# Attention with a soft mixture of experts on one core: the order of two key transfers in the last batch, and the tile at which one weight unit is sent for

## The chip, the cores and the metric

The kernel runs on one core of one Trainium2 chip. The metric is the device time of one execution in microseconds (us), lower is better. The time before is the median of three runs, 250.34 us (247.84 to 250.55). The profile comes from a further, profiled execution that has a time of its own, 251.09 us.

## The reference

Windowed causal attention (window 128, linear bias by head) over 8 batches, 8 heads, 576 positions and head size 64; its output, seen as 4608 tokens of 512 features, goes through a soft mixture of 8 experts with 4 slots each.

```python
scores = scale * np.matmul(q, k.transpose(0, 1, 3, 2))
mask = (rel >= 0) & (rel < window)
scores = np.where(mask, scores + bias[None], -1000000000.0)
attn = np.exp(scores - max); attn = attn / (sum + 1e-09)
x = (attn @ v) as [tokens, heads * head_dim]
logits = x @ phi                       # 4608 x 32
d = softmax of logits over the tokens; slot_input = d.T @ x
slot_out[e] = relu(slot_input[e] @ w1[e]) @ w2[e]     # 8 experts, F = 1024
out = (softmax of logits over the slots) @ slot_out
```

## The kernel before

The work is cut into 36 tiles of 128 tokens. A batch of 576 positions has four tiles `t` = 0 to 3 of 128 queries, and the 64 queries left over of two neighbouring batches make a fifth, `t` = 4. So even batches have four tiles and odd ones five. Tiles are counted here from 0 in the order in which they run: tile 10 is the eleventh and belongs to batch 2, tiles 31 to 35 are those of the last batch (batch 7), which runs in the order `t` = 1, 4, 2, 3, 0. Batch 0 starts at tile 0, batch 1 at 4, batch 2 at 9, batch 3 at 13, batch 6 at 27.

One pass of the main loop, "period k", works on several tiles at once. TensorE (PE) transposes the probabilities of tile k-1 (L319) and the finished tokens of tile k-3 (L387), multiplies tile k-2 by its values (L355, L367), and ends with the scores of tile k+1 (L263). The scores come in two halves `g` = 0 and 1, each with 16 matmuls and a PSUM buffer of its own. VectorE (DVE) merges the window (L277), finds the row maxima into `nb` (L286), and divides by the row sums (L378, L381). ScalarE (ACT) does the exponentials (L301) and copies out of PSUM (L322, L390). GpSimd (POOL) cuts the window's corners (L339, L342). Every fourth tile the logits and the running slot sums are added (L400, L438, L450).

All loads of the main loop are issued by SyncE (SP) in one hand-written order. An issue waits for the buffer it writes to be free and for the transfer eight places ahead of it to have landed, and what stands behind a waiting issue waits too. In period k SP gets, in this order:

- `weights(k)`: units of expert weights, 512 KB each, 64 in all, from tile 3 on. Ahead of each unit `hold` issues a 4-byte transfer into `beat` that reads the row maxima `nb` of one half of tile k, so the unit can't leave before DVE has them. Tiles in `BOTH` send for two units, one behind each half; the others for one, behind the first half, or the second if they are in `LATE`.
- `after_values(k-2)`: loads of values (`va`) into slots that PE has just freed.
- `loads(k+1)`, behind the scores of tile k+1: the queries (`q_t`) of tile k+3, and part of the keys (`k_t`). Keys come in blocks of 64 positions, 128 KB each; `k_part(b, i, e)` loads blocks i to e-1 of batch b, and there are `NB` = 9 in a batch.

In the last batch the second half of tile 32 (`t` = 4) reads blocks 6, 7 and 8, and tile 33 (`t` = 2) reads blocks 2 to 5. The kernel before sends for blocks 4 and 5 in `loads(30)` and for blocks 6 to 8 in `loads(31)`.

Behind the main loop the slots' inputs go through the experts: `hidden` (L774) with the first 32 units, `experts` (L810) with the other 32, and `combine` (L831, L837) writes the output. Of the 64 units 38 go behind holds; the other 26 are sent for at the end of the loop and in the tail.

Of the kernel before, what the change touches and what calls it, by code (L numbers as in the profile page):

```python
# [37 lines left out]
NB = S // KB  # L38
# [7 lines left out]
GAPS = (1, 3)  # L46
WFIRST = 3
LATE = (4, 5, 21, 25, 29, 30)
BOTH = (31, 32, 33, 34, 35)
CUTS = (0, 128, 256, 384, 512)  # L50
NM = len(CUTS) - 1
MW = [CUTS[m + 1] - CUTS[m] for m in range(NM)]
# [15 lines left out]
def tile_attn_softmoe(  # L68
# [74 lines left out]
    def hold(ap):  # L143
        i = len(held)
        held.append(ap)
        nc.sync.dma_start(beat[0:1, i:i + 1], ap[0:1, 0:1])

    def load_weight():
        n = loaded[0]
        loaded[0] += 1  # L150
        m, e, k = units[n]
        if NW <= n < NW + len(place):
            wt[units[n]] = place[n - NW]
        else:
            wt[units[n]] = wpool.tile([P, UW], F32, tag="w", name=f"w{n}")
        nc.sync.dma_start(wt[units[n]], (w1d, w2d)[m][e, :, UW * k:UW * (k + 1)])

    st = {}
    last = B - 1
# [403 lines left out]
    def k_part(b, i, e):  # L563
        return (load_k, (b, i, e))

    def loads(k):
        b, t = tiles[k]
        now = []
        if k + 2 < n:
            now.append((load_q, (k + 2,)))  # L570
        if k < 4:
            now.append((load_v, ()))
        if t == 0 and 0 < b < last:
            now.append(k_part(b, 4, 6))
        if t == 1:
            now.append(k_part(b, 6, NB))
        if b % 2 == 0 and t == 2:
            now.append(k_part(b + 1, 0, 2))
        if b % 2 == 0 and (t == 3 if b + 1 < last else t == 2):
            now.append(k_part(b + 1, 2, 4))  # L580
        if b + 1 == last and t == 3:
            now.append(k_part(last, 4, 6))
        if b % 2 and b < last and t >= 3:
            now.append(k_part(b + 1, 2 * t - 6, 2 * t - 4))
        issue(now)
# [11 lines left out]
    def issue(items):  # L597
        for fn, a in items:
            fn(*a)

    def weights(k):
        gates = (0, 1) if k in BOTH else (k in LATE,)
        for g in gates if k >= WFIRST else ():
            hold(st[k, g]["nb"])
            load_weight()

    for q in range(NQ - 1):
        k = 4 * q + 6
# [13 lines left out]
    with tc.manual_schedule(engines=ORDERED):  # L622
        scores(0, 0)
        idle_work(GAPS[0])
        scores(0, 1)
        loads(0)
        for k in range(n):
            if k:
                chain(k, 0)
            else:  # L630
                for us in (LO, HI):
                    merge(k, 0, us)
                    rowmax(k, 0, us)
                    expo(k, 0, us)
            chain(k, 1)
            weights(k)
            for _ in range(2):
                filler()
# [32 lines left out]
            if k + 1 < n:  # L671
                scores(k + 1, 0)
                scores(k + 1, 1)
                loads(k + 1)
# [312 lines left out]
```

## Time and profile before

| | us |
|---|---|
| median of three runs | 250.34 |
| lowest and highest | 247.84, 250.55 |
| the profiled execution, its own time | 251.09 |
| span of its instructions | 249.4 |
| PE busy in the span | 234.5 |
| DVE, ACT, POOL busy | 176.8, 165.6, 94.5 |

The 1.7 us between own time and span lie around the program. In the profile an instruction's row has its start, how long it took, engine, line, tiles, and in brackets how long its engine sat idle before it and what ended that by the profile. "SPq" rows are issues of transfers. A share of the DMA is the mean busy share of 16 DMA engines in a stage.

### The profile page before, as it was taken

How to read it: one execution, taken by the hardware profiler on the slowest of the kernel's cores; microseconds unless marked ns; L12 is line 12 of the kernel's file. 1: busy time of each engine (PE TensorE's matmuls, PEld its weight loads, DVE VectorE, ACT ScalarE, POOL GpSimd, SP SyncE). 2: the span in 40 equal slices, each digit the busy share in tenths (PEclk: the TensorE clock that was granted, in tenths of full speed). 3: DMA queues.
4: the chain of work that ended last, by engine and by line, in shares of the span. 5: the costliest groups of instructions: out<-in, count | busy, mean ns of one | idle time of the engine just before them, and what ended most of it. 6: DMA issues, size and time to landing. Idle time of an engine off the chain costs nothing. (4 is left out here: it accounts for less than half of the span.)

```text
span 249.4 us, 12344 instructions
## 1 busy us (share of the span) xinstructions
PE 234.5 (94%) x4867; PEld 175.6 (70%) x4868; DVE 176.8 (71%) x971; ACT 165.6 (66%) x473; POOL 94.5 (38%) x235
## 2 busy tenths in 40 slices
PE   6989999998999999999999999979997999999982
PEld 2668887886788778787788788768876423766640
DVE  0787888986998898798798899778886412244451
ACT  2698987987888888797797979849762310033441
POOL 2038455723651765086077608537550010000000
PEclk9999999999999999999999999999999999999985
DMA  6798887796897588888876989988899999977997
GB/s 175 250 289 273 264 315 216 257 335 216 273 297 255 167 292 262 292 287 252 298 230 212 288 239 330 303 314 293 257 329 369 409 408 410 407 277 307 354 387 277
DMA packets 28505, 72.72 MB, mean 292 GB/s; under 512 B 3358, under 2 KB 3872, under 8 KB 28448
## 3 DMA queue, kind: packets, MB, share of 16 engines
q1 hardware_dynamic: 27728, 71.11, 83.1%
q10 hardware_dynamic: 720, 0.84, 1.2%
q8 instruction: 38, 0.62, 1.0%
q14 instruction: 19, 0.16, 0.2%
HBM read 62.49 MB, written 9.44 MB: 288 GB/s over the span
## 5 line engine op out<-in xcount | busy, mean ns | idle before, releaser
L301 ACT ACTIVATE area<-sq,nb 128x128 f32<-128x128 f32 x288 | 89.4, 400 | 4.0 <-DVE nb L286 2.9
L342 POOL TENSOR_SCALAR_AFFINE_SELECT area<-area 64x256 f32<-64x256 f32 x112 | 46.3, 413 | 85.3 <-ACT area L322 76.9
L286 DVE CUSTOM_DVE_ANT_0 sq<-s,cst 128x128 f32<-128x128 f32 x224 | 51.8, 287 | 7.7
L322 ACT COPY area<-pt 128x512 f32<-128x512 f32 x71 | 41.9, 593 | 20.6 <-PE pt L319 17.6
L263 PE MATMUL s<-kq 64*64 64x192 f32 (+2 forms) x1152 | 51.6, 310 | 3.6 <-DVE nb L286 2.1
L339 POOL TENSOR_SCALAR_AFFINE_SELECT area<-area 64x256 f32<-64x256 f32 x112 | 45.5, 416 | 5.8
L263 PEld LDWEIGHTS s<-kq 64*64 64x64 f32 x1152 | 39.6, 135 | 9.4 <-DVE nb L286 3.8
L319 PE MATMUL pt<-unit_r,area 128*128 128x128 f32 x288 | 44.3, 278 | 0.0
L355 PE MATMUL xp<-va,area 128*64 128x65 f32 x1120 | 41.1, 224 | 1.3 <-issue 1.3
L355 PEld LDWEIGHTS xp<-va,area 128*64 128x64 f32 x1120 | 35.9, 137 | 7.5 <-issue 5.8
L319 PEld LDWEIGHTS pt<-unit_r,area 128*128 128x128 f32 x288 | 32.2, 140 | 7.1 <-ACT area L301 4.6
L277 DVE COPY_PREDICATED s<-cst,s 128x256 f32<-128x256 int32 (+1 forms) x73 | 30.6, 419 | 6.7 <-PE s L263 6.6
L381 DVE TENSOR_TENSOR xs<-xp,rs 128x256 f32<-128x256 f32 x70 | 26.6, 420 | 1.2
L390 ACT COPY xs<-xq 128x512 f32<-128x512 f32 (+1 forms) x36 | 20.9, 585 | 6.0 <-PE xq L387 5.8
L286 DVE DVE_READ_ACCUMULATOR2_ANT nb<- 128x1 f32 x288 | 23.8, 83 | 0.0
L387 PE MATMUL xq<-unit_r,xs 128*128 128x128 f32 x142 | 21.9, 278 | 1.2 <-DVE xs L381 0.9
L837 DVE COPY ob<-po 128x384 f32<-128x384 f32 x24 | 12.5, 554 | 13.7 <-PE po L831 12.9
L367 PEld LDWEIGHTS xp<-va,area 64*64 64x64 f32 x864 | 15.2, 133 | 7.4 <-issue 6.4
L837 ACT COPY ob<-po 128x384 f32<-128x384 f32 x24 | 10.5, 481 | 14.0 <-PE po L831 13.9
L367 PE MATMUL xp<-va,area 64*64 64x65 f32 x864 | 19.0, 224 | 0.0
L387 PEld LDWEIGHTS xq<-unit_r,xs 128*128 128x128 f32 x142 | 15.9, 141 | 3.3 <-PE pt L319 2.4
L286 DVE CUSTOM_DVE_ANT_0 sq<-s,fine 128x128 f32<-128x128 f32 x64 | 14.9, 287 | 1.9
(109 smaller groups left out, 232.8 us busy)
## 6 DMA issues: line engine op xcount, KB each, us to landing
w<-w SPq DMA_DIRECT2D x48, 512.0 KB
out<-ob SPq DMA_DIRECT2D x24, 384.0 KB
kq<-q_t SPq DMA_DIRECT2D x34, 256.0 KB
va<-v_n SPq DMA_DIRECT2D x32, 260.0 KB
kq<-k_t SPq DMA_DIRECT2D x24, 256.0 KB
kq<-k_t SPq DMA_DIRECT2D x8, 384.0 KB
kq<-w SPq DMA_DIRECT2D x4, 512.0 KB
area<-w SPq DMA_DIRECT2D x4, 512.0 KB
```

Of the source, the lines that this page charges most:

```text
L263: nc.tensor.matmul(parts[par][half[c], jh, KB * o:WIN], lhsT=qt[rows, j], rhs=keys[rows, i:i + 3 - o, j], start=(t > 0 and jh == 0), stop= ...
L277: nc.vector.copy_predicated(window(k, g, us, 0, KB), bc(mask_le, 1, len(range(4)[us])), window(k, g, us, P, KB))
L286: nc.vector.tensor_tensor_reduce(out=s["sq"][:, u], in0=window(k, g, u, 0, P), in1=bias[:, u] if tiles[k][1] else zero.to_broadcast([P, P] ...
L301: nc.scalar.activation(dst, s["sq"][:, u].rearrange("p (a w) -> p a w", a=2), AF.Exp, bias=s["nb"][:, u:u + 1], scale=-1.0)
L319: nc.tensor.transpose(s["pt"][:, u], s["p4"][:, u], ident)
L322: copy(pas[k % 2][:, g].rearrange("p a j m -> p (a j m)"), st[k, g]["pt"].rearrange("p u w -> p (u w)"))
L339: nc.gpsimd.affine_select(dst, pa, [[0, NPAIR], [-1, KB]], ALU.is_gt, 0.0, base=0, channel_multiplier=1)
L342: nc.gpsimd.affine_select(dst, pa, [[0, NPAIR], [1, KB]], ALU.is_ge, 0.0, base=0, channel_multiplier=-1)
L355: nc.tensor.matmul(x[par][half[g], j], lhsT=pas[k % 2][:, g, par, j], rhs=v[:, par, j], start=(j == 0), stop=(t == 0 and j == NPAIR - 1))
L367: nc.tensor.matmul(x[par][half[g], j], lhsT=pps[k % 2][rows, g, j], rhs=v, start=False, stop=(j == NPAIR - 1))
L381: nc.vector.tensor_tensor(x[:, par], xp[par][:, :, 0:D], bc(rs[:, par], 2, D), op=ALU.mult)
L387: nc.tensor.transpose(st["xq", k][:, P * j:P * j + P], xns[k % NXN][:, P * j:P * j + P], ident)
```

## The change

Two things are edited, each in a rule that sets SP's order. Nothing else changes: the instructions of PE, DVE, ACT and POOL stand in the same order as before, and the 64 weight units come in the same order.

```diff
 LATE = (4, 5, 21, 25, 29, 30)
-BOTH = (31, 32, 33, 34, 35)
+NONE = (10,)
+BOTH = (12, 31, 32, 33, 34, 35)
...
         if t == 1:
-            now.append(k_part(b, 6, NB))
+            now.append(k_part(b, 6, NB) if b < last else k_part(b, 4, 6))
...
         if b + 1 == last and t == 3:
-            now.append(k_part(last, 4, 6))
+            now.append(k_part(last, 6, NB))
...
     def weights(k):
         gates = (0, 1) if k in BOTH else (k in LATE,)
-        for g in gates if k >= WFIRST else ():
+        for g in gates if k >= WFIRST and k not in NONE else ():
             hold(st[k, g]["nb"])
             load_weight()
```

Since a line is added at the top, lines of the changed kernel behind it have numbers that are one higher.

**First place, SP from period 10 to period 12.** `beat` and `w_` are a hold and its unit, `va` values, `q_t` queries, `k_t` keys (128x512 is two blocks, 128x768 three). Before:

```order
L146 DMA beat<-nb 1x1
L156 DMA w_1128<-w 128x1024
L197 DMA va<-v_n 128x520 x2
L180 DMA kq<-q_t 128x512
L187 DMA kq<-k_t 128x512
L146 DMA beat<-nb 1x1
L156 DMA w_1252<-w 128x1024
L204 DMA va<-v_t 128x520
L180 DMA kq<-q_t 128x512
L187 DMA kq<-k_t 128x512
L146 DMA beat<-nb 1x1
L156 DMA w_1357<-w 128x1024
```

Now:

```order
L198 DMA va<-v_n 128x520 x2
L181 DMA kq<-q_t 128x512
L188 DMA kq<-k_t 128x512
L147 DMA beat<-nb 1x1
L157 DMA w_1249<-w 128x1024
L205 DMA va<-v_t 128x520
L181 DMA kq<-q_t 128x512
L188 DMA kq<-k_t 128x512
L147 DMA beat<-nb 1x1
L157 DMA w_1354<-w 128x1024
L147 DMA beat<-nb 1x1
L157 DMA w_1357<-w 128x1024
```

The first hold and unit (period 10) are gone from the top; period 12 ends with two holds and two units in place of one. From there on SP is level with the kernel before.

**Second place, SP from `loads(30)` to the weights of period 31**, with the semaphores that each issue waits for. Before:

```order
L180 DMA kq<-q_t 128x512 [waits DMAHW3_49,PE_49]
L187 DMA kq<-k_t 128x512 [waits DMAHW4_49]
L146 DMA beat<-nb 1x1 [waits DMAHW5_49,DVE_49]
L156 DMA w_3415<-w 128x1024 [waits DMAHW6_49]
L197 DMA va<-v_n 128x520 [waits DMAHW7_49,PE_49]
L180 DMA kq<-q_t 128x512 [waits DMAHW0_49,PE_49]
L187 DMA kq<-k_t 128x768 [waits DMAHW1_49]
```

Now:

```order
L181 DMA kq<-q_t 128x512 [waits DMAHW3_49,PE_49]
L188 DMA kq<-k_t 128x768 [waits DMAHW4_49]
L147 DMA beat<-nb 1x1 [waits DMAHW5_49,DVE_49]
L157 DMA w_3415<-w 128x1024 [waits DMAHW6_49]
L198 DMA va<-v_n 128x520 [waits DMAHW7_49,PE_49]
L181 DMA kq<-q_t 128x512 [waits DMAHW0_49,PE_49]
L188 DMA kq<-k_t 128x512 [waits DMAHW1_49]
```

The three blocks and the two blocks have changed places. A transfer signals on the semaphore of the one whose place it takes, so the three blocks signal on DMAHW1 before and on DMAHW4 now.

**Third place, PE at the scores of tiles 32 and 33** (`s_0` and `s_1` are the two halves). Before:

```order
L263 MATMUL s_0_87<-kq 64x192 [waits DMAHW3_49,DVE_49]
L263 MATMUL s_0_87<-kq 64x192 x7
L263 MATMUL s_1_88<-kq 64x192 [waits DMAHW1_49,DVE_49]
...
L263 MATMUL s_0_87<-kq 64x192 [waits DMAHW4_49,DMAHW0_49,DVE_49]
L263 MATMUL s_0_87<-kq 64x192 x7
L263 MATMUL s_1_88<-kq 64x192 [waits DVE_49]
```

Now:

```order
L264 MATMUL s_0_87<-kq 64x192 [waits DMAHW3_49,DVE_49]
L264 MATMUL s_0_87<-kq 64x192 x7
L264 MATMUL s_1_88<-kq 64x192 [waits DMAHW4_49,DVE_49]
...
L264 MATMUL s_0_87<-kq 64x192 [waits DMAHW1_49,DMAHW0_49,DVE_49]
L264 MATMUL s_0_87<-kq 64x192 x7
L264 MATMUL s_1_88<-kq 64x192 [waits DVE_49]
```

The matmuls are the same. The second half of tile 32 waits for the three blocks in both, and the first half of tile 33 for the two; only the transfers behind those semaphores have changed places.

## The prediction

> **What bounds the kernel now.** I read the page first, then the chain that ended last, then the places where TensorE (PE) sits idle.
>
> ```profile
> span 249.4 us, 12344 instructions
> PE 234.5 (94%) x4867; PEld 175.6 (70%) x4868; DVE 176.8 (71%) x971; ACT 165.6 (66%) x473; POOL 94.5 (38%) x235
> ```
>
> PE is busy for 94% of the span; no other engine passes 71%. So a change of SP's order can only matter where PE waits for what SP brings. The chain, in order of time, names the waits that are left:
>
> ```profile
> 163.77 0.34 DVE s L277
> ...
> 164.53 0.02 DVE nb L286
> 164.54 0.11 issue
> 164.65 0.88 PE s L263 x16
> ...
> 187.47 1.26 issue
> ```
>
> From 164.65 to the end it is nearly all PE, with one larger hole, 1.26 us from 187.47. That hole has no releaser: the profile knows no engine and no transfer that PE waited for. Ahead of the chain's first PE row lies the first stall that concerns this change, in PE's timeline:
>
> ```profile
> 162.23 0.83 PE L263 MATMUL s<-kq 64*64 64x192 f32 x16
> 164.65 0.88 PE L263 MATMUL s<-kq 64*64 64x192 f32 x16 [1.59 <-DVE nb L286]
> ...
> 168.52 1.48 PE L263 MATMUL s<-kq 64*64 64x192 f32 x32
> ```
>
> These are the scores of tile 32, first half, second half, and then both halves of tile 33. Between the halves PE idles 1.59 us. The profile puts it down to DVE, but the rows speak against that. The second half writes the buffer whose last reader was the row maximum of tile 31, and DVE had that long before:
>
> ```profile
> 160.76 0.08 DVE L286 DVE_READ_ACCUMULATOR2_ANT nb<- 128x1 f32 x1
> ...
> 153.92 0.33 SPq L187 DMA_DIRECT2D kq<-k_t  x1
> 158.66 0.69 SPq L187 DMA_DIRECT2D kq<-k_t  x1
> ```
>
> The order of PE (third place above) lists one more condition for exactly this matmul, DMAHW1, and DMAHW1 is the transfer of blocks 6 to 8, issued at 158.66. It was 164.65 - 158.66 = 5.99 us on its way when PE went on. The transfer of blocks 4 and 5 left at 153.92, though nothing reads it before 168.52. I take the 1.59 us as a wait for keys.
>
> The other larger stall in the loop is at tile 11, behind the place where the weight unit goes away:
>
> ```profile
> 53.23 0.36 SPq L156 DMA_DIRECT2D w<-w  x1
> ...
> 54.53 0.08 DVE L286 DVE_READ_ACCUMULATOR2_ANT nb<- 128x1 f32 x1
> ...
> 55.26 0.83 PE L263 MATMUL s<-kq 64*64 64x192 f32 x16
> 57.16 0.88 PE L263 MATMUL s<-kq 64*64 64x192 f32 x16 [1.07 <-DVE s L277]
> ```
>
> Again PE stops between two halves, for 1.07 us. Here the matmul has no transfer among its conditions, only DVE, whose last maximum of the buffer's old tile is at 54.53. So like the 1.26 us at 187.47 this is a hole without a stated cause. One thing does reach PE by transfers and has no semaphore in the program, its instructions:
>
> ```profile
> q8 instruction: 38, 0.62, 1.0%
> ```
>
> 0.62 MB in 38 pieces for 4867 + 4868 PE instructions are 16 KB and 256 instructions a piece. A piece that lands late would look just like these two holes. That is my reading; no view here shows which piece was late.
>
> [...]
>
> **Part one, the keys.** The three blocks leave at 153.92 in place of 158.66. If they take the same 5.99 us they are there at 159.91, and PE asks for them at 164.65 - 1.59 = 163.06: 3.1 us to spare, so the 1.59 us go. The two blocks leave at 158.66; with 5.99 us for a smaller load, 164.65 at the latest, and tile 33 asks for them at 168.52 - 1.59 = 166.93: 2.3 us to spare, cost nothing.
>
> What is late next? The other engines at this place:
>
> ```profile
> 165.59 0.43 DVE L277 COPY_PREDICATED s<-cst,s 128x256 f32<-128x256 int32 x1 [0.42 <-PE s L263]
> ...
> 168.73 0.24 DVE L378 TENSOR_SCALAR rs<-xp 128x4 f32<-128x4 f32 x2 [1.13 <-PE xp L367]
> ...
> 166.21 0.59 ACT L322 COPY area<-pt 128x512 f32<-128x512 f32 x1 [3.41 <-PE pt L319]
> ```
>
> When PE comes 1.59 us sooner, DVE has 0.42 + 1.13 = 1.55 us of idle time to follow, ACT 3.41. So DVE is level with PE behind this place, and 1.55 us are the gain that can pass on.
>
> Then the transfers. The holds of periods 32 to 35 follow DVE, the queries and values follow PE, so all of them are asked for up to 1.55 us sooner. The stages show whether the DMA engines can take that:
>
> ```profile
> 160.00:165.00 5.00, 3.41 (x93) 2.16 (x92) 3.92 (x23) 2.80 (x9) 2.84 (x7) 1.00 0.96 353
> 165.00:170.00 5.00, 5.00 (x124) 4.16 (x117) 3.22 (x19) 3.79 (x12) 2.80 (x7) 1.00 0.77 249
> 170.00:175.00 5.00, 5.00 (x114) 4.43 (x114) 4.51 (x28) 4.18 (x13) 3.79 (x10) 1.00 0.93 315
> ...
> 185.00:190.00 5.00, 3.74 (x103) 3.23 (x102) 3.65 (x13) 0.58 (x1) 0.25 (x1) 1.00 1.03 379
> ```
>
> The last two columns are the DMA's share and its GB/s. From 165 to 170 it is idle for 0.23 x 5 = 1.15 us; on either side it is nearly full. So 1.15 us of the shift find room, and 1.55 - 1.15 = 0.40 us turn into a longer queue for what PE needs next, its instructions above all. Bounds: nothing is given back (the queue's growth falls on weights that are wanted much later), or all 1.55 are, in the hole at 187.47, where the share is 1.03. I take 0.40, nearer to the first bound, since only this part finds no room. The 128 KB that stand earlier in the queue between 153.92 and 158.66 cost at most 128 KB / 353 GB/s = 0.37 us to what is behind them; keys and queries have over 2 us to spare there, so I take 0, and 0.37 as the end. Part one: -1.55 + 0.40 = -1.15 us, between -1.59 and +0.37.
>
> **Part two, the weight unit.** A hold and a unit leave period 10, and come behind the unit of period 12. What this takes from the DMA at 53 to 60 us and adds from 66 us on is 512 KB, at the 315 GB/s of a full stage 1.66 us.
>
> ```profile
> 50.00:55.00 5.00, 5.00 (x124) 4.16 (x120) 4.51 (x28) 4.04 (x12) 1.64 (x4) 1.00 0.95 339
> 55.00:60.00 5.00, 3.93 (x89) 3.10 (x81) 4.18 (x26) 3.28 (x11) 0.41 (x1) 1.00 0.77 256
> ...
> 65.00:70.00 5.00, 4.69 (x132) 3.99 (x130) 4.62 (x28) 4.49 (x13) 3.93 (x10) 1.00 0.92 261
> 70.00:75.00 5.00, 4.91 (x122) 4.05 (x119) 4.59 (x27) 4.20 (x13) 2.17 (x6) 1.00 0.99 315
> 75.00:80.00 5.00, 5.00 (x125) 4.22 (x122) 4.35 (x27) 4.16 (x14) 0.15 (x1) 1.00 0.77 259
> 80.00:85.00 5.00, 5.00 (x86) 3.58 (x88) 3.79 (x22) 3.94 (x12) 3.30 (x9) 1.00 0.49 157
> ```
>
> Gain: at most the 1.07 us at 57.16. I expect none of it. [...]
>
> Cost: the new pair of issues is like the first two rows here, and stands behind them and ahead of the next three on SP; the last row is PE at the scores of tile 15.
>
> ```profile
> 64.58 0.58 SPq L146 DMA_DIRECT2D beat<-nb  x1
> 65.20 0.39 SPq L156 DMA_DIRECT2D w<-w  x1
> 66.55 0.33 SPq L197 DMA_DIRECT2D va<-v_n  x1
> 67.50 0.46 SPq L180 DMA_DIRECT2D kq<-q_t  x1
> 68.02 0.43 SPq L187 DMA_DIRECT2D kq<-k_t  x1
> ...
> 76.81 1.48 PE L263 MATMUL s<-kq 64*64 64x192 f32 x32
> ```
>
> Hold and unit take 0.58 + 0.39 = 0.97 us of SP, so the values leave about 1 us later and the keys about 0.5 us (SP waited for PE ahead of the queries anyway). Tile 15 asks for keys and queries at 76.81, 8.3 us behind the new issue; 5.99 us, the long way that we saw, plus 1.66 is 7.65. It is covered, and the added queue is worked off from 75 to 85, where the DMA idles 0.23 x 5 + 0.51 x 5 = 3.7 us. Without that cover a piece of instructions behind the doubled units would be up to 1.66 us late. Part two: 0, between -1.07 and +1.66.
>
> **Sum.** -1.15 + 0 = -1.15 us. Against the profiled execution's own 251.09 that is 249.94; the median shown is 0.75 us lower, so I forecast 250.34 - 1.15 = **249.2 us**, 0.5% faster, too little to be told from no change at 1%, which is about what a measurement of this kernel can tell.
>
> **Rivals.**
>
> - *All is given back.* PE comes sooner to the unexplained hole at 187.47 and waits there longer; the 1.03 share speaks for it, the idle 1.15 us from 165 on against it. Time 250.3.
> - *Both stalls go.* The hole at 57.16 hangs on the unit at 53.23 after all; its place right behind the unit speaks for it, its missing transfer condition against. -1.59 - 1.07 = -2.66: 247.7.
> - *The swap doesn't remove the stall*, since DVE ended it, as the profile says. The maximum at 160.76 and the DMAHW1 condition speak against. Time 250.3.
> - *Slower.* Instruction pieces queue behind bulk data, and two units in one period push one over its slack: +1.66 us at about 70 to 80, where the share is 0.99. It decides when a piece has less than 1.66 us to spare. With the gain at tile 32 handed back by the same mechanism the time is 250.34 + 1.66 = 252.0.
>
> [...]
>
> [...]
>
> **Chances.** Forecast 0.36; nothing given back 0.16; all given back 0.18; both stalls go 0.15; stall stays 0.07; slower 0.08. The three runs shown spread over 2.7 us, so each case carries about a microsecond of scatter. Faster by over 1% means below 247.84: over half of "both stalls", and a little of the others, 0.16. Slower by over 1% means above 252.84: part of the last rival, 0.04. Within 1%: 0.80. The range 246.9 to 250.9 takes in "both stalls" with scatter and "all given back", and leaves out most of the slower rival; the likeliest case's own range is 248.7 to 250.0.
>
> **What would show it.** Right: no idle time between the halves of tile 32's scores; DVE's idle 0.42 and 1.13 there nearly gone; the hole near 57 still there, about 1.07; the hole near 187 grown by some tenths; no new hole from 66 to 85. Wrong: the idle time at tile 32 still there (not the keys), or a hole near 57 that is gone (then the unit was its cause), or a new one of a microsecond or more between 66 and 85 or between 167 and 187.

## The result, and the profile after

The changed kernel takes 252.15 us in the median of 22 runs (249.24 to 258.43), the kernel before 250.95 us in 22 runs on the same chip (247.84 to 254.11). The ratio is 1.0067, with a 95% interval of 1.0038 to 1.0095: slower by two thirds of a per cent. A second comparison of the same kernel later gave 1.0048 [1.0004, 1.0092]. Runs of one kernel differ by about 2 us (one standard deviation), so several kernels below cannot be told from no change by their time alone, and I read their traces stage by stage instead. The ratios leave out runs more than 1.5% above the fastest of their own kernel, which in the second comparison kept 10 of 12 runs of the change but 16 of 35 of the kernel before and so leans towards slower; where I give means, they are over all runs. By those means the two comparisons gave +1.6 and -0.4 us, each with a standard error of 0.6, together +0.6 (0.4). So there is a small loss by the ratios, and by the means it is not clear of zero.

The page of the changed kernel's profiled execution, whose own time is 252.01 us, begins:

```profile
span 250.3 us, 12346 instructions
PE 236.3 (94%) x4868; PEld 176.2 (70%) x4868; DVE 176.5 (71%) x971; ACT 165.6 (66%) x473; POOL 94.5 (38%) x235
```

The span is 0.9 us longer than before and PE's share is the same. The two key transfers in question leave SP at 155.00 and 159.57; the earlier is now that of blocks 6 to 8 (SP's timeline):

```profile
155.00 0.33 SPq L188 DMA_DIRECT2D kq<-k_t  x1
...
159.57 0.43 SPq L188 DMA_DIRECT2D kq<-k_t  x1
```

PE's timeline at the scores of tiles 32 and 33, which answers to the rows at 162.23, 164.65 and 168.52 of before:

```profile
163.50 1.48 PE L264 MATMUL s<-kq 64*64 64x192 f32 x32
164.92 0.66 PE L320 MATMUL pt<-unit_r,area 128*128 128x128 f32 x4
...
167.97 1.32 PE L264 MATMUL s<-kq 64*64 64x192 f32 x28
```

All 32 matmuls of tile 32 now stand in one row: nothing waits between the halves. The idle 1.59 us are gone, and tile 33 begins 4.47 us after tile 32 where it took 168.52 - 162.23 = 6.29 us. DVE's idle 0.42 us ahead of the masked copy and 1.13 us ahead of the next scaling are gone too, in the same two rows of DVE's timeline:

```profile
166.36 0.42 DVE L278 COPY_PREDICATED s<-cst,s 128x256 f32<-128x256 int32 x1
...
168.28 0.22 DVE L379 TENSOR_SCALAR rs<-xp 128x4 f32<-128x4 f32 x2
```

So the change does what it says at its place. In PE's list of waits one row has grown from 1.3 us and one time (before) to this:

```profile
PE xp L356 <- issue: 2.8, 4, 1.2
```

"Issue" means that the profile knows nothing that PE waited for. Three of the four stand here, in PE's timeline; the fourth, 0.80 us at 26.32, lies ahead of both edits:

```profile
80.29 0.97 PE L356 MATMUL xp<-va,area 128*64 128x65 f32 x25
81.56 0.45 PE L356 MATMUL xp<-va,area 128*64 128x65 f32 x7 [0.30 <-issue]
...
181.28 0.74 PE L356 MATMUL xp<-va,area 128*64 128x65 f32 x18
182.50 0.51 PE L356 MATMUL xp<-va,area 128*64 128x65 f32 x9 [0.47 <-issue]
...
187.28 0.45 PE L356 MATMUL xp<-va,area 128*64 128x65 f32 x6
188.92 1.03 PE L356 MATMUL xp<-va,area 128*64 128x65 f32 x26 [1.18 <-issue]
```

The last is the hole of before (there 1.26 us, after the same sixth matmul). The other two are new, and so is the one at 26.32. That one alone is nearly the 0.9 us by which the two spans differ, so this pair of profiles can't show where the time went. PE stops in the middle of 32 like matmuls, each time ahead of one that by the profile waits for no semaphore. The hole at 81 lies some 15 us behind the added weight unit, the one at 182 some 19 us behind the stall that is gone.

The stages at these places, in the windows' columns of before (last two: the DMA's share, GB/s):

```profile
65.00:70.00 5.00, 4.68 (x123) 3.95 (x124) 4.62 (x28) 4.49 (x14) 3.95 (x10) 1.00 0.82 262
70.00:75.00 5.00, 4.91 (x122) 4.06 (x120) 4.59 (x29) 4.21 (x13) 2.48 (x7) 1.00 0.95 340
75.00:80.00 5.00, 5.00 (x135) 4.41 (x132) 4.36 (x27) 4.15 (x14) 0.00 (x0) 1.00 0.93 318
...
165.00:170.00 5.00, 5.00 (x114) 4.43 (x115) 4.51 (x27) 4.09 (x12) 3.27 (x8) 1.00 0.86 293
170.00:175.00 5.00, 5.00 (x115) 4.43 (x114) 4.60 (x31) 4.28 (x12) 3.37 (x9) 1.00 0.99 326
```

From 75 to 80 the share rises from 0.77 to 0.93, from 165 to 170 from 0.77 to 0.86, and from 170 to 175 from 0.93 to 0.99. The idle time of the DMA that the prediction counted on was in part filled (from 165 to 170 us, 0.7 of 1.15 us are left). Whether that was free is the question of what follows.

### The profile page after: what moved, and what is told of

Its sections match the earlier page's. It is cut to its first block, busy times and chain, and to the rows that moved or that the text cites. A ratio compares the mean times of both kernels' runs of the same rounds, so it can differ in the third digit from the quotient of the medians.

```text
span 250.3 us, 12346 instructions
## 1 busy us (share of the span) xinstructions
PE 236.3 (94%) x4868; PEld 176.2 (70%) x4868; DVE 176.5 (71%) x971; ACT 165.6 (66%) x473; POOL 94.5 (38%) x235
## 5 line engine op out<-in xcount | busy, mean ns | idle before, releaser
L356 PE MATMUL xp<-va,area 128*64 128x65 f32 x1120 | 41.8, 224 | 3.4 <-issue 2.8
L838 ACT COPY ob<-po 128x384 f32<-128x384 f32 x24 | 10.3, 482 | 14.5 <-PE po L832 14.5
```

Of the source, the lines that this page charges most:

```text
L356: nc.tensor.matmul(x[par][half[g], j], lhsT=pas[k % 2][:, g, par, j], rhs=v[:, par, j], start=(j == 0), stop=(t == 0 and j == NPAIR - 1))
```

## The theory and its rivals

**Theory: late instructions.** PE's instructions come in pieces of 16 KB (before's instruction queue: 38 transfers, 0.62 MB), which for 4867 matmuls and 4868 weight loads are 256 instructions a piece. By the theory a piece that stands behind bulk data comes late. The change puts bulk data ahead of pieces at two places: a second weight unit at period 12, and, behind tile 32, the same transfers asked for sooner. It gains about 1.2 us around tile 32 and pays for it in small holes elsewhere.

**Rival one: the order itself.** The holds, the places on SP or the swap cost something whatever the traffic is. **Rival two: chance.** The holes fall where they fall, and the change moves only which of them are seen.

Two readings of the trace carry the theory. First, I numbered all of PE's instructions of each profile (matmuls, weight loads and PE's sequencer's) by start time and took the number of the instruction behind each hole. Between 15 and 237 us, in all 18 profiles of this case, every hole over 0.1 us whose releaser is "issue" has a number that leaves 192, 193 or 194 when divided by 256. So has the hole near 57 us, for which the profile names DVE in various ways. Stalls with a releaser of their own do not: in before, 114 for the 1.59 us and 128, 132 and 240 for the waits on DVE's "xs".

Second, the 38 transfers of the instruction queue can be put against PE. The fetch of a piece begins when PE enters the piece ahead of it (in the profiles of before and after 0.43 us sooner at the earliest) or, mostly, well after: by 2.1 and 2.2 us in the mean of pieces 1 to 30. Where PE stops for it, PE mostly goes on 2.2 to 2.7 us after the fetch began: in 71 of the 75 holes of over 0.1 us that stand at such a number in the 18 profiles. The other four take 3.0 to 4.3 us, and there the fetch itself took 1.5 to 2.8 us, not about 0.95. Counted from the end of the fetch, PE goes on 1.25 to 1.75 us later in all 75, those near 57 us included. So a fetch ends these holes, whatever the profile names. I call the time from PE's entering the piece ahead to the start of the fetch the delay.

```
                         before                        after
piece  PE enters   fetch starts  delay    PE enters   fetch starts  delay   hole ahead of the piece
       piece ahead                        piece ahead                       (before / after)
 10       70.04        71.16      1.13       70.43        73.37       2.94   none / none
 11       75.44        76.55      1.11       75.83        79.13       3.31   none / 0.30 at 81.56
 29      177.35       179.94      2.59      177.04       180.25       3.21   none / 0.47 at 182.50
 30      182.29       186.12      3.83      182.50       186.20       3.70   1.26 / 1.18
```

Without its holes PE takes 4.9 to 5.4 us for the piece ahead of each of these in before. By my estimate from that and the 2.2 to 2.7 us above, a delay of up to some 2.7 us is hidden, and what goes beyond it stops PE. Pieces 10 and 11, with 1.1 us of delay, were far from that line in the profile of before; in that of after they reach it. What a fetch waits for during its delay no row of the profile names. That it is bulk data is what the experiments have to show.

## The experiments

**One: the keys alone.**

```
+NONE = ()
-            now.append(k_part(b, 6, NB))
+            now.append(k_part(b, 6, NB) if b < last else k_part(b, 4, 6))
-            now.append(k_part(last, 4, 6))
+            now.append(k_part(last, 6, NB))
```

> Only the two key transfers change places; the weight units stay as before. Theory (PE loses time where a 16 KB piece of its instructions lands late behind bulk transfers): the 1.59 us between the halves of tile 32's scores go, small holes near 160 and from 176 to 189 us grow by 0.5 to 1.0 us together, ratio 0.995 to 0.999. Rival (the swap itself is the loss, since the three blocks now stand ahead of everything in a full stage): ratio 1.003 or more. Rival (nothing is given back): ratio 0.993 to 0.994.

Measured: 252.31 us (12 runs) beside 251.79 (29 runs), ratio 0.9966 [0.9906, 1.0027], a mean of +1.0 us (standard error 0.8). The time decides nothing. In the trace the stall at tile 32 is gone, the holes near 81 are not there, and the later ones are (PE's timeline, near 183 us and in the output projection):

```profile
181.54 0.91 PE L356 MATMUL xp<-va,area 128*64 128x65 f32 x23
183.26 0.46 PE L356 MATMUL xp<-va,area 128*64 128x65 f32 x9 [0.81 <-issue]
...
224.05 0.28 PE L811 MATMUL op<-sq,ht 128*8 128x128 f32 x1 [0.42 <-issue]
```

So in this profile the hole near 182 comes with the keys and the one near 81 does not. It is not the swap's own, though: eight and twelve below have it with the keys of before (1.57 us at 182.52, 0.53 at 182.72), and in both the stall at tile 32 is gone or short.

**Two: the weight unit alone.**

```
-BOTH = (31, 32, 33, 34, 35)
+NONE = (10,)
+BOTH = (12, 31, 32, 33, 34, 35)
```

> Only the weight unit moves from tile 10 to tile 12; the keys stay as before. Theory: the doubled units make pieces of instructions late between 70 and 85 us, one or two new holes of 0.3 to 0.8 us there, the 1.59 us at tile 32 stay; ratio 1.002 to 1.008. Rival (the move is hidden and the loss of the whole change is the swap's): ratio 0.998 to 1.002, no new hole from 66 to 85 us. Rival (the hole near 57 us hangs on the unit at tile 10): that hole is gone and the ratio is 0.995 to 0.998.

Measured: 253.24 us, ratio 0.9976 [0.9924, 1.0028], mean +1.1 (0.8). The ratio missed the theory's range, and the hole near 57 us is not gone (1.36 us at 55.90). Two holes in its PE timeline tell more:

```profile
79.28 0.57 PE L356 MATMUL xp<-va,area 128*64 128x65 f32 x13
80.43 0.45 PE L356 MATMUL xp<-va,area 128*64 128x65 f32 x7 [0.57 <-issue]
...
162.83 0.83 PE L264 MATMUL s<-kq 64*64 64x192 f32 x16
165.11 0.88 PE L264 MATMUL s<-kq 64*64 64x192 f32 x16 [1.44 <-DMA kq<-k_t]
```

The hole near 81 comes with the weight unit. And the stall at tile 32, kept here since the keys are as before, is now put down to the key transfer. The same matmul waits for nearly the same time in both profiles, and in this one the transfer is named.

**Three: the unit three periods later still**, to period 15, keys as before.

```
-BOTH = (31, 32, 33, 34, 35)
+NONE = (10,)
+BOTH = (15, 31, 32, 33, 34, 35)
```

> The unit of tile 10 is sent with that of tile 15, where the transfer engines idle half of the time (share 0.49 from 80 to 85 us), in place of tile 12; the keys stay as before. Theory: no hole from 66 to 80 us, and at most a small one from 82 to 90; ratio 0.998 to 1.002, below the one of tile 12. Rival (where the unit is put makes no difference): the same ratio as with tile 12, within 0.002.

Measured: 251.4 us, ratio 1.0053 [1.0012, 1.0095], mean +0.6 (0.65). No hole from 66 to 85 us, where the whole change and the second kernel have one. Yet the ratio is above what was expected, and no better than theirs. Its holes are elsewhere (2.09 us at 52.10, 0.74 at 92.03, 0.50 at 121.06), and some of these places have holes in other kernels too. So the place of the hole follows the unit; that the loss goes with it is not borne out by this run.

**Four: 36 more PE instructions at the start**, nothing else.

```
-        idle_work(WARM)
+        idle_work(WARM - 2)
+        for _ in range(20):
+            nc.tensor.matmul(idle_bank[:, 0:16], lhsT=warm[:, 0:P], rhs=warm[:, 0:16], start=True, stop=True)
```

> The kernel before with 36 more PE instructions ahead of the first tile (two of the 7 warm-up matmuls give way to 20 small ones), so that pieces of 256 instructions end 36 instructions earlier in the program; no transfer is moved. Theory: the hole of 1.26 us behind the sixth matmul of the values of tile 34 moves 36 instructions up in the program, to among the corner matmuls (64x65) of tile 33 or just ahead of them, and is 0.8 to 1.7 us long. Rival (the hole belongs to something that this matmul waits for): it stays behind the sixth matmul of tile 34's values.

Measured: 255.61 us in one run. PE's timeline of it, and that of before at the same tile:

```profile
190.18 0.57 PE L369 MATMUL s<-va,area 64*64 64x65 f32 x21
191.48 0.45 PE L369 MATMUL s<-va,area 64*64 64x65 f32 x11 [0.73 <-issue]
```

```profile
187.02 0.45 PE L355 MATMUL xp<-va,area 128*64 128x65 f32 x6
188.73 0.97 PE L355 MATMUL xp<-va,area 128*64 128x65 f32 x26 [1.26 <-issue]
```

Before, the hole comes after the sixth matmul of the values of tile 34. With 36 instructions ahead, it comes 17 matmuls sooner: 6 of that group and 11 of the group ahead of it, which with their weight loads make 34 instructions (an instruction of PE's sequencer stands among them). It did not stay with its tile and its operands. This is the run that shows the cause of these holes: a place in the stream of instructions, not a place in the work. It speaks against a semaphore or a buffer as the cause.

**Five and six: less bulk data.** Every second weight unit of the first 35 is not loaded, in the kernel before and in the changed one.

```
+        if n < NW and n % 2:
+            wt[units[n]] = wt[units[n - 1]]
+            return
```

> The kernel before, with every second of the 35 weight units of the main loop left out (the unit ahead of it is used in its place, so part of the computation is changed); 17 transfers of 512 KB fewer, PE's work is the same. Theory (late pieces of PE's instructions behind bulk transfers): no hole without a stated cause of over 0.2 us between 20 and 180 us in the profile, the 1.59 us at tile 32 gone or under 0.5 us since the keys come sooner, ratio 0.984 to 0.993, runs closer together (middle half within 1.5 us). Rival (the holes and the scatter have nothing to do with the transfers): holes of 0.3 to 2 us remain in the loop, ratio 0.995 or more.

> The same half of the weight units left out of the changed kernel. Theory: both edits act through the load on the transfer engines, so with the load gone this and the kernel before with the same half left out are equal: ratio 0.984 to 0.993, within 0.003 of each other, no hole near 81 us and none from 174 to 184. Rival (the order of the issues itself costs SP or PE something): this one stays 0.004 or more above the other.

Measured: the first 250.59 us (10 runs) beside 252.69 (29 runs), ratio 0.9976 [0.991, 1.0043], mean -1.9 (0.6). The second has four times (246.43 to 251.42), too few for a ratio. The ratio missed what was expected, the median and the mean did not, and I took the pair again at more runs (below). The holes without a cause from 50 to 100 us are gone in both profiles. The one near 187 us is not: 1.72 us at 187.28 in the first, 0.91 at 183.66 in the second. It lies where the last units stream, which these kernels load in full. The first also has 0.27 us at 25.23 and 0.84 at 159.73, where none over 0.2 us was expected, and its runs did not come as close together as expected (the middle half is some 3 us wide).

**Seven and eight: room ahead of tile 32.** The units of periods 29 and 30 are loaded at 15 and 25; seven with the swapped keys, eight with the keys of before.

```
-BOTH = (31, 32, 33, 34, 35)
+NONE = (29, 30)
+BOTH = (15, 25, 31, 32, 33, 34, 35)
```

> The two key transfers change places, and the units of tiles 29 and 30 (full stages from 150 to 160 us) are sent with those of tiles 15 and 25 (stages with a share of 0.49 and 0.71); tile 10 keeps its unit. Theory: the gain at tile 32 stays, since the queue behind it is 1 MB shorter: no hole from 155 to 180 us, ratio 0.990 to 0.996. Rival (the gain is handed back whatever stands in the queue, since the last units and the tail set the end): 0.998 to 1.003.

> The same move of the units of tiles 29 and 30 to tiles 15 and 25, with the keys as before. Theory: the three key blocks come 1 to 2 us sooner since a unit of 512 KB ahead of them is gone, so the 1.59 us at tile 32 shrink to 0 to 0.6; ratio 0.991 to 0.997, within 0.003 of the one with the swap. Rival (the stall at tile 32 does not depend on the queue): it stays at 1.4 to 1.6 us, ratio 0.999 or more.

Measured: seven 252.38 us, ratio 1.0057 [1.0004, 1.0111]; eight 251.65, ratio 1.0002 [0.9933, 1.007], beside 252.69. Eight's PE timeline at tile 32:

```profile
162.22 0.70 PE L368 MATMUL xp<-va,area 64*64 64x65 f32 x32
162.73 1.48 PE L264 MATMUL s<-kq 64*64 64x192 f32 x32
```

The stall is gone without the swap, with a 512 KB unit taken out of the queue ahead of the keys. So it was the keys, and it was the queue. But neither kernel brought the gain that was expected. By the ratio eight is no faster (its mean is 0.8 us lower, standard error 0.6): behind tile 32 it has holes of 1.57 us at 182.52 and 0.36 at 188.12, where before has 1.26 in all. In this profile the gain at tile 32 is handed back without the swap, too.

**Nine, ten, eleven: the change, its keys and its weight unit once more**, in one comparison beside 35 runs of the kernel before (252.31 us). The edits are those of the change, of one and of two.

> The whole change once more, beside its two halves on one chip, since what the halves cost does not yet add up to what the whole did. Theory (both halves act through late pieces of PE's instructions, each by some tenths of a microsecond, the rest of the 0.67% is scatter): ratio 1.000 to 1.006; the idle time between the halves of tile 32 gone; every hole of PE that has no stated cause stands at the same place of a 256-instruction period as in the earlier profiles. Rival (the two edits together cost what neither costs alone): 1.006 or more, and over both halves by 0.006.

> The key transfers alone, on the same chip. Theory: most of the 1.59 us is handed back by holes between 170 and 195 us that are together 0.8 us or more longer than in kernels that keep the stall; ratio 0.996 to 1.002. Rival (nothing is given back): 0.992 to 0.995.

> The weight unit alone (tile 10 to tile 12), on the same chip. Theory: a hole of 0.3 to 0.8 us near 80 us again, as in both profiles with this edit so far; ratio 1.001 to 1.004. Rival (that hole was chance): no hole from 70 to 85 us, ratio 0.998 to 1.001.

Measured: the change 251.88 us, ratio 1.0048 [1.0004, 1.0092]; the keys 252.3, 1.0029 [0.9976, 1.0083]; the unit 251.99, 1.006 [1.0018, 1.0103]. The change is slower again by the ratio, not by the mean. One and ten together, weighted by their intervals, put the keys at 1.000 (standard error 0.002), two and eleven the unit at 1.003 (0.002). Two and eleven are one kernel, though, and 0.9976 and 1.006 differ by two and a half times the error of such a difference, so these errors are too small. By the means over all runs the keys are at +0.5 us (0.6) and the unit at +0.4 (0.5). Ten missed its expectation: its holes between 170 and 195 us are 0.85 us together, where before has 1.26 and two 0.54. Eleven's ratio is above its range. Here are the holes behind the moved unit, in PE's timeline of nine and then of eleven:

```profile
80.81 0.86 PE L356 MATMUL xp<-va,area 128*64 128x65 f32 x23
81.98 0.45 PE L356 MATMUL xp<-va,area 128*64 128x65 f32 x7 [0.30 <-issue]
```

```profile
75.12 0.43 PE L401 MATMUL lp<-xs,phi 128*32 128x128 f32 x8
75.86 0.86 PE L401 MATMUL lp<-xs,phi 128*32 128x128 f32 x24 [0.32 <-issue]
```

Eleven stops one piece sooner than nine. Which of the two pieces is caught varies; that one is, does not, in the four profiles that have this edit. Ten has neither.

**Twelve: two units moved**, from periods 9 and 10 to 12 and 13, keys as before.

```
-BOTH = (31, 32, 33, 34, 35)
+NONE = (9, 10)
+BOTH = (12, 13, 31, 32, 33, 34, 35)
```

> The suspected cost doubled: tiles 9 and 10 send for no unit, tiles 12 and 13 for two each; keys as before. Theory: the stages from 65 to 80 us are full, pieces of instructions are late there more than once, holes of 0.8 us or more together between 66 and 86 us; ratio 1.003 to 1.008. Rival (the units' place costs nothing): holes under 0.3 us there, ratio 0.998 to 1.002.

Measured: 252.41 us, ratio 1.0062 [1.0015, 1.011]. It has no hole at 75 to 82 us but two later (0.31 at 92.00, 0.56 at 97.52), and no full stall at tile 32 either. Doubling the edit did not double the loss. This run bears on the theory only in that its pieces 10 and 11 are late (3.30 and 2.50 us).

**Thirteen to sixteen: the change and its halves with half of the bulk data**, each with the three lines of five. This is the test of rival one.

> The kernel before with every second of the first 35 weight units not loaded (17 units of 512 KB left out, their weights are those of the unit ahead, so this part of the computation is changed). It is the base for the next three kernels, at more rounds than its first time, when it took 250.59 us beside 252.69. Theory (instruction pieces wait behind bulk data, 1 to 2 us of an execution): 1.5 to 2.5 us faster than the kernel before, ratio 0.990 to 0.994. Rival (the bulk data costs PE nothing, the holes lie where they lie): ratio 0.999 to 1.001.

> The whole change on that base (17 units left out, weights changed). Theory: with the bulk data out of the way the change does what it was read to do, so it is 0.8 to 1.6 us faster than the base (ratio lower by 0.003 to 0.006), where with all units it was 0.6% slower. Rival (the loss is not a matter of bulk data but comes with the order itself): slower than the base by 0.004 to 0.007.

> Only the keys changed, on that base (17 units left out, weights changed). Theory: 0.8 to 1.6 us faster than the base, like the whole change there. Rival (the gain at tile 32 is handed back whatever the bulk data): level with the base within 0.002.

> Only the weight unit moved, on that base (17 units left out, weights changed; which of the two moved units are loaded follows their number, so here one unit at most is moved and no period holds two loads). Theory: no hole at 75 to 82 us and level with the base within 0.002. Rival (the move costs by its holds and its order on SP, not by its data): slower than the base by 0.002 to 0.004.

Measured beside 251.73 us (35 runs):

| kernel, half of the units | median us | mean us (standard error) | ratio to before |
|---|---|---|---|
| thirteen, orders of before | 249.31 | 249.27 (0.28) | 0.9939 [0.9901, 0.9978] |
| fourteen, whole change | 249.19 | 249.39 (0.50) | 0.9928 [0.9886, 0.9971] |
| fifteen, keys | 249.89 | 249.75 (0.29) | 0.9957 [0.9919, 0.9995] |
| sixteen, weight unit | 250.14 | 250.19 (0.30) | 1.0 [0.996, 1.0041] |

The base comes out as the theory expected: 17 units less are worth 0.6% by the ratio and 2.4 us by the medians. So bulk data does cost time, which rival two denies; that all of it is late pieces is not shown, since the stall at tile 32 went with it. That the change would gain 0.8 to 1.6 us on it was wrong, and I can see why: PE's timeline of thirteen has no stall at tile 32 to be gained.

```profile
162.89 1.48 PE L266 MATMUL s<-kq 64*64 64x192 f32 x32
164.30 0.66 PE L322 MATMUL pt<-unit_r,area 128*128 128x128 f32 x4
```

With nothing to gain and room in the queue, the whole change is level (+0.1 us, standard error 0.6), which is neither the theory's gain nor rival one's loss. In fourteen no period loads two units (the second one of period 12 is among those left out), so what is tested is the order without the doubled load. The stages there have room, and there is no hole without a cause from 68 to 92 us:

```profile
70.00:75.00 5.00, 4.90 (x123) 4.05 (x116) 4.59 (x29) 4.20 (x13) 1.43 (x4) 1.00 0.91 308
75.00:80.00 5.00, 5.00 (x131) 4.30 (x122) 4.35 (x27) 4.16 (x14) 0.83 (x2) 1.00 0.45 128
```

Sixteen, 0.9 us above its base (standard error 0.4), missed its expectation in time and met that of rival one, while its trace has no hole at 75 to 82. Its weight half costs nothing when joined with the keys (fourteen less fifteen: -0.4 us). I leave it open.

At one boundary less data did not help. Near 57 us thirteen to sixteen have holes of 1.37, 0.80, 2.09 and 1.63 us, and the delay of that piece, piece 7, is 3.6 to 4.8 us, though none of them loads a unit in period 10. With all data it is 1.2 to 4.4 us; five, the same kernel as thirteen, has 2.2 and no hole. Over pieces 1 to 30 the mean delay is 2.3 us in the twelve kernels with all data and 1.7 in the six with half. So bulk data lengthens the delays on the whole, and it is not all that they are made of.

**All profiles side by side.** These are stages between the first score matmuls of tiles, us, with the delays of the pieces fetched there. Kernels with the same state of an edit are listed together. Four is left out, since its pieces end elsewhere in the program, and so are five and six, which thirteen and fourteen repeat.

```
                                     13 to 18   delay of pieces 10, 11
unit at 10, all data   before          25.00      1.13 1.11
                       one             25.00      1.87 1.55
                       ten             25.00      2.08 2.32
                       seven, eight    24.86 24.74    1.67 2.46, 1.38 2.20
unit at 12, all data   after           25.56      2.94 3.31
                       nine            25.56      2.99 3.21
                       two             26.08      3.41 3.42
                       eleven          25.51      3.60 1.95
                       twelve          25.39      3.30 2.50
unit at 15, all data   three           24.38      2.16 1.93
half of the data       13 14 15 16     24.76 25.02 24.77 24.77   0.46 to 1.82

                                     29 to 33   33 to 35   35 to end  delay of 34, 35
stall kept, all data   before          21.52      10.25      70.61     1.55 1.07
                       two             21.37      10.11      69.62     2.36 0.85
                       eleven          21.17      10.28      69.67     2.33 0.92
                       three, twelve   21.06 20.56  10.12 10.41   70.26 70.52   2.62 0.92, 2.16 1.37
keys swapped, all data after           20.22      10.52      71.80     3.37 2.85
                       nine            20.26      10.59      69.49     2.77 2.11
                       one             20.04      10.99      71.93     3.83 2.19
                       ten             19.97      10.81      71.49     3.99 2.02
                       seven           20.05      10.66      70.49     3.03 2.60
keys old, stall gone   eight           20.05      10.21      71.64     2.65 2.11
half of the data       13 14 15 16     20.16 20.04 20.43 20.11  10.12 10.12 10.12 10.30  70.69 69.97 71.16 70.30
```

The stage 13 to 18 is a steady one. With the unit at 10 it takes 24.92 us in the mean of five profiles, with the unit at 12 it takes 25.62, and the two groups do not overlap. With half of the data both orders take 24.8 to 25.0. So the weight move costs **0.7 us** in this stage, and it costs it by its data: rival one falls here.

Tile 32's region, 29 to 33, is 1.2 us shorter with the keys swapped (20.11 in the mean) than where the stall stands in full (21.35: before, two, eleven). Then 33 to 35 takes 10.71 with the keys swapped and 10.23 where the keys are old (without eight), again with no overlap, and 10.1 to 10.3 with half of the data, swapped or not. So **0.5 us** go back before tile 35, by the data again. (Four, with the keys of before, takes 11.74 there, with holes of 0.23 and 0.91 us at its own boundaries.) From tile 35 to the end the swapped kernels take 71.0 and the others (without eight) 70.1, **0.9 us** more; the swapped ones scatter by 1 us, and with half of the data there is no such difference. With a standard error of 0.5 this last number is not clear of chance. Part of it is the hole near 187, which scatters in both groups. The other part can be followed: from the first to the last matmul of `experts` (L810), after, one and ten take 0.5 to 1.1 us longer than the rest of the table, whose times agree within 0.25 us. They are the three whose piece 34, fetched in that stretch, has a delay of over 3.3 us; in all others it is 3.0 or less. Pieces 34 and 35 together have 5.8 us of delay in the mean of the swapped kernels and 3.2 in the others, without overlap.

The sum: -1.2 + 0.5 + 0.9 = +0.2 for the keys (standard error some 0.5, nearly all of it from the last stage), +0.7 for the unit, +0.9 us in all. The two comparisons of the whole change gave 0.5% and 0.7% by the ratio, 1.2 to 1.7 us, and +1.6 and -0.4 us by the means. What is left over is within the scatter of the stages from 18 to 29, where holes of 0.3 to 1.5 us come and go in kernels of every kind. This is seven's, in its PE timeline:

```profile
94.81 0.69 PE L368 MATMUL xp<-va,area 64*64 64x65 f32 x31
96.99 0.21 PE L368 MATMUL xp<-va,area 64*64 64x65 f32 x1 [1.49 <-issue]
```

Rival two is right to that extent: one profile of one kernel shows by chance a microsecond more or less. It is wrong for 13 to 18 and for 33 to 35, where the groups do not overlap.

No kernel here is faster than the kernel before beyond the scatter, but for those that leave loads out.

## Why the prediction was wrong, point by point

It forecast 249.2 us, 0.5% faster; the result is 0.5 to 0.7% slower by the ratios, and 252.15 us lies outside its range. The step that failed first is **part two: "0, between -1.07 and +1.66"**.

**The stall at tile 32: right.** It was a wait for keys, against the name in the profile; the swap took it away in all five kernels that have it, and a lighter queue took it away too (eight). The prediction's sign for it was that the second half writes a buffer that DVE had long left, and that the transfer's semaphore is among the matmul's conditions.

**"-1.55 us pass on": right at its place.** From tile 32 to tile 33 the five swapped kernels take 4.47 us and those with the full stall 5.94 to 6.29, which is 1.5 to 1.8 us. That 29 to 33 got shorter by only 1.2 us comes from just ahead of it: between tiles 30 and 32 the swapped kernels take 11.55 to 11.84 us, before, two and eleven 11.26 to 11.28. In four of the five there is a wait of 0.16 or 0.17 us for DVE's "xs" near 154 us (156 in nine), which three and eight have as well, so it is not the swap's. After and ten also have a hole at a piece boundary (0.11 us at 160.91, 0.21 at 161.10).

**"0.40 given back": right for the place it looked at, and too small by the rest.** From 33 to 35 it was 0.5. The working took the DMA's idle 1.15 us as room for the shift, and the trace of after shows it partly filled. But more may go back past tile 35: 0.9 us (standard error 0.5) to the end, of which the 0.5 to 1.1 us behind piece 34 in three of five kernels are the part that can be followed. The gain was asked about at one stage only. What was lost fits the mechanism that it named, "a longer queue for what PE needs next, its instructions above all".

**Part two: "0": wrong, +0.7 us.** The cover that it worked out was right for what it covered: keys and queries of tile 15 were not late (no idle time ahead of its scores, at 76.81 us before and 77.20 in after). It then said that without that cover a piece of instructions behind the doubled units would be up to 1.66 us late, and took nothing, since the DMA has idle time from 75 to 85. Pieces 10 and 11 came late all the same. The number to take was a piece's slack: PE takes some 5 us for a piece, and where it waits 2.2 to 2.7 us pass from fetch to first instruction, so by that estimate some 2.7 us of delay are hidden. Pieces 10 and 11 had 1.1 us of delay in the profile of before; 512 KB more ahead of them, 1.66 us by the prediction's own estimate, makes 2.8 us, at the edge. They measured 2.9 and 3.3 in after. One profile would not have been enough to tell, though: with the unit at 10 other kernels show 1.4 to 2.5.

**The slower rival came nearest**, in both of its parts (the piece behind two units, and the gain handed back by the same mechanism). It got 0.08. Its price of +1.66 was too high for part two. That its time, 252.0, is nearly the one that came is luck in part: it was counted from 250.34, and the kernel before took 250.95 beside the change. What kept its chance low was the wish to see a single piece with less than 1.66 us to spare; the 1.07 us at 57.16 and the 1.26 us at 187.47 were two that had none, and they were quoted.

**The hole near 57: half right.** It did not hang on the unit at 53.23: with the unit moved it is 1.36 us in two (at 55.90) and absent in "after" and nine, and with the unit in place it is 1.63 us in ten and absent in one; and it is there in thirteen to sixteen, which load no unit in period 10. But the forecast that it stays at 1.07 us took a chance event for a fixed one. The same goes for the hole near 187: none in twelve, 0.3 us in nine and eleven, 1.26 before, 1.73 in fifteen. Why part two should gain none of the 1.07 us no run shows: in the profile of before the fetch that ends this hole starts at 54.80, after the unit left SP at 53.23.

**"Nothing given back", 0.16 of the chances.** No run shows it, and none shows a reason for it. They show 0.5 us handed back from 33 to 35. And at pieces 10 and 11 the delay is 1.1 to 2.5 us with one unit, 2.0 to 3.6 with two, 0.5 to 1.8 with half of the data: there more bulk data ahead makes the fetch later. Why piece 7 is no sooner with half of the data, no run here shows.

**The median.** The 250.34 us that the forecast was taken from was the median of three runs; 22 runs gave 250.95, and the four later comparisons 251.7 to 252.7. The chance of "within 1%" held: 0.80, and the ratio is within it.

## What to carry to other kernels

Where an engine runs close to full and the DMA too, count its instructions among what a transfer can make late (here 512 KB more went with a delay of 2.9 us for piece 10 in after, 1.1 before): find the pieces' boundaries, and for each the time between its fetch and its first instruction; a transfer moved ahead of a piece with little to spare can cost time (here 0.7 us from 13 to 18). Before a gain is booked, ask what of it is handed back at every busy DMA stage to the end, not only the next. And where runs differ by 2 us, one trace's hole proves little; the same stage of many kernels, grouped by the edit, tells a few tenths.

## What the runs showed of the hardware that was not expected

- A fetch of 16 KB of instructions mostly takes about 0.95 us (0.88 to 2.81), where PE waits for it PE goes on 1.25 to 1.75 us after it ends, and it mostly starts 0.5 to 4.8 us after PE enters the piece ahead. Most of the 37 crossings from one piece to the next cost nothing here, and the others cost 1 to 6 us together in an execution (0.91 in six, 5.8 in four), up to 2.09 us at one boundary (three, at 52.10; fifteen at 57.44).
- Such a hole can be named for an engine. Near 57 us the profiles name DVE's "s", "nb" or "xs" for it, though its number in PE's stream is 193 or 194 of 256 in each. The hole of 0.74 us at 92.03 in three, number 192, is named for DVE's "rs". The stall at tile 32 is named for DVE before (1.59 us) and for the key transfer in two (1.44 us).
- With less bulk data the runs were faster and mostly steadier: the standard deviation is 1.0 us in thirteen, fifteen and sixteen and 1.7 in the 35 runs of before beside them, but also 1.7 in fourteen.
